# Order of the bias factors, key casts and band copies, and the number of output buffers, in a T5 attention + maxout FFN kernel

## The chip, the cores and the metric

The kernel runs on one core of a Trainium2 chip. The metric is the device time of one execution in microseconds (us). Before the change the median of three executions is 356.96 us, the lowest 355.21 and the highest 357.01.

Names used: PE is TensorE (matmuls and transposes), DVE is VectorE, ACT is ScalarE, POOL is GpSimd, SP is SyncE. SP, ACT and POOL also issue DMAs. PSUM is the memory that matmuls write; SBUF is the working memory.

## The reference

```python
def _attn_ref(q, k, v, bias_table):            # q, k, v: (8, 8, 576, 64) f32, bias_table: (32, 8)
    scores = (1.0 / np.sqrt(D)) * np.matmul(q, k.transpose(0, 1, 3, 2))
    bucket = ...                               # of |i - j|: 0..15 one each, then logarithmic up to 128, then 31
    scores = scores + bias_table[bucket].transpose(2, 0, 1)[None]
    attn = np.exp(scores - np.max(scores, axis=-1, keepdims=True))
    attn = attn / (np.sum(attn, axis=-1, keepdims=True) + 1e-09)
    return np.matmul(attn, v)

def reference(...):
    x = attn_out.transpose(0, 2, 1, 3).reshape(B * S, H * D)          # 4608 x 512
    h = np.maximum(np.maximum(x @ w1, x @ w2), x @ w3)                # 4608 x 768
    return h @ w_out                                                  # 4608 x 512
```

The bias depends on the head and on the distance of query and key alone, and is one constant per head from a distance of about 128 on.

## The kernel before

**The work.** There are 8 batches of 8 heads with 576 queries and keys. Heads go in pairs (`hp` 0 to 3), since two heads of 64 fill the 128 partitions. Keys are cut into 4 blocks of 128 and a rest of 64; queries into two halves of 256 and a rest of 64. One "visit" of a pair and a half (`visit`) makes 8 score matmuls (`sc<-qT,kT`) and two exponentials on ACT (`e<-sc`). `left_keys` (`sct`) and `left_queries` (`scq`) do the rests. `attend` multiplies the exponentials with the values (`a<-vx,e`), and its inner function `quotients` divides by the row sums on DVE and writes `x_sb`.

**The bias.** Instead of adding a bias, the kernel multiplies the exponentials by a factor, exp(bias - last bias), which is 1 away from the diagonal. The 32 x 8 table comes in over ACT's queue as `tableT`; DVE negates its last column (`negc`), ACT makes the factors `etab`, and 17 small DVE copies spread them over `w_sb`, one row per head. ACT stores `w_sb` to DRAM as `w_dr`, and SP reads it back with one shifted row per partition: two loads `hank` (heads 0 to 3, then 4 to 7) and four small ones `hankt`. `make_band` copies a pair's part of `hank` in reverse into `band`; `times_band` multiplies the exponentials near the diagonal by it, three DVE instructions per pair in the first half. `bands(hp)` does both for the first half of batch 0.

**The first batch.** The keys of batch 0 come in f32: heads 0 and 1 (pair 0) over ACT's queue, with the table between the two, heads 2 to 7 over SP's. `cast_keys(hp)` turns a pair's keys to bf16 on DVE. `first_transposes(hp)` transposes the pair's first queries and its keys on PE into a PSUM tile `tp`, and copies them out to `qT` and `kT` (DVE, but ACT for `qT` of pair 0). The first loop over `hp` visits the first query half of each pair and, from pair 1 on, queues the bands of the pair before; at pair 3 it also runs the first `attend`. The second loop visits the second half of batch 0. Then come batches 1 to 7, with two visits per pair.

**The FFN between.** `ffn` cuts a block of 512 tokens into portions of matmuls which `fill` places between the visits of the following batch, so that PE has work while ACT computes exponentials. A portion's three products go to PSUM banks `ps`, are reduced by a maximum (ACT copies the first one, DVE does the two maxima) into `hT`, and `output` multiplies `hT` by `w_out` into a bank `pso`. All of `ps`, `pso` and the transposes of batch 0 share the two banks of the pool `ps_f`. DVE copies `pso` into an SBUF tile `osb` (line 339), whose pool `osbp` has 3 buffers, and SP stores `osb` (line 343). The stores are held back in a list and issued by `store_outputs` after the next visit, so on SP's queue they stand among the DMA transposes of that place (line 405 for the next batch's queries and keys, line 565 for `x_sb`). A block has four outputs, so four copies and four stores.

**What sets the order.** Each engine runs its instructions in one fixed order. Calls wrapped in `inorder` keep the order of the program; for the others a scheduler places the instruction by its priority. DVE, ACT and SP each work through their list strictly: an instruction that waits holds up all behind it.

```python
    osbp = ctx.enter_context(tc.tile_pool(name="osbp", bufs=3))                      # line 83
    load_32(k, 0, k32, nc.scalar)
    inorder(nc.scalar.dma_start(out=tableT[:], in_=tbl_src))                         # line 193
    load_32(k, 1, k32, nc.scalar)
    last_keys = first_transposes(0)
    inorder(nc.scalar.dma_start(out=w_dr[:], in_=w_sb[:]))                           # line 598
```

Of the kernel before, what the change touches and what calls it, by code (L numbers as in the profile page):

```python
# [39 lines left out]
def kernel(  # L40
# [12 lines left out]
    nc = tc.nc  # L53
# [6 lines left out]
    HP = H // 2  # L60
# [19 lines left out]
    nrm = ctx.enter_context(tc.tile_pool(name="nrm", bufs=3))  # L80
    xs = ctx.enter_context(tc.tile_pool(name="xs", bufs=2))
    ffnw = ctx.enter_context(tc.tile_pool(name="ffnw", bufs=2))
    osbp = ctx.enter_context(tc.tile_pool(name="osbp", bufs=3))
    ps_s = ctx.enter_context(tc.tile_pool(name="ps_s", bufs=2, space=bass.MemoryType.PSUM))
    ps_a = ctx.enter_context(tc.tile_pool(name="ps_a", bufs=2, space=bass.MemoryType.PSUM))
    ps_f = ctx.enter_context(tc.tile_pool(name="ps_f", bufs=2, space=bass.MemoryType.PSUM))
# [4 lines left out]
    inorder = tc.keep_in_program_order  # L91
# [4 lines left out]
    def tr(*args):  # L96
        inorder(nc.tensor.transpose(*args))
# [14 lines left out]
    def act_copy(out_, in_):  # L112
        inorder(nc.scalar.activation(out=out_, in_=in_, func=ACTF.Copy))

    def dve_copy(out_, in_):
        inorder(nc.vector.tensor_copy(out_, in_))  # L116
# [10 lines left out]
    def main_part(src, b):  # L127
        return src[b, :, 0 : KT * P, :].rearrange("h (t p) d -> p t h d", p=P)
# [30 lines left out]
    def load_q(b, h0, h1):  # L159
        load_main(q, b, h0, h1, batch[b][0])  # L160
        load_tail(q, b, h0, h1, q_diag)
# [13 lines left out]
    def borrow(c, n):  # L175
        return xT[:, c, NTOK - 2 * n :].bitcast(F32)

    k32 = borrow(3, KT * H * D).rearrange("p (t h d) -> p t h d", t=KT, h=H)
    q32 = borrow(2, 2 * 2 * D).rearrange("p (t h d) -> p t h d", t=2, h=2)

    def load_32(src, h, dst, eng, nt=KT):
        inorder(eng.dma_start(out=dst[:, :, h, :], in_=main_part(src, 0)[:, 0:nt, h, :]))
# [7 lines left out]
    batch[0] = load_tiles()  # L190
    w_sb = stage.tile([H, WL], BF16, name="w_sb")
    load_32(k, 0, k32, nc.scalar)
    inorder(nc.scalar.dma_start(out=tableT[:], in_=tbl_src))
    load_32(k, 1, k32, nc.scalar)
    nc.scalar.preload_act_table_set("natural_log_exp_and_others")
    for h in range(2):
        load_32(q, h, q32, nc.sync, 2)
    for h in range(2, H):
# [16 lines left out]
        out=negc[:], in0=tableT[:, NB - 1 : NB], scalar1=-1.0, scalar2=None, op0=ALU.mult,  # L215
# [8 lines left out]
    def cast_keys(hp):  # L224
        h = slice(2 * hp, 2 * hp + 2)
        dve_copy(batch[0][1][:, :, h, :], k32[:, :, h, :])
# [5 lines left out]
        mm(warm[:, 0:CH], lhsT=qtail[1][:, 0, :], rhs=qtail[1][:].rearrange("p g c -> p (g c)"))  # L232

    act_copy(batch[0][0][:, 0:2, 0:2, :], q32)
    cast_keys(0)
    dve_copy(w_sb[:, HALF : HALF + single], etab[:, 0:single])
    reach = single
    for vv, rg in enumerate(ranges):
# [7 lines left out]
    w_dr = dram.tile([H, WL], BF16, name="w_dr")  # L246
# [15 lines left out]
    def make_band(hp):  # L262
        dve_copy(band[hp][:], hank[:, 2 * hp : 2 * hp + 2, ::-1])
# [148 lines left out]
    def qk_tiles():  # L412
        return [qkt.tile([P, HP, (KT + 1) * P], BF16, tag=n, name=n) for n in ("qT", "kT")]

    def first_transposes(hp):


        hs = slice(2 * hp, 2 * hp + 2)
        tp = ps_f.tile([P, 2 * CH], BF16, tag="ff", name="tp1")
        K, L = KT * P, KT * P + P  # L420
        for t in range(2):
            tr(tp[:, L + P * t : L + P * t + P], batch[0][0][:, t, hs, :].rearrange("p h d -> p (h d)"), ident[:])
        for t in range(KT):
            tr(tp[:, P * t : P * t + P], batch[0][1][:, t, hs, :].rearrange("p h d -> p (h d)"), ident[:])
        if hp:
            tr(tp[:, K:L], ktail[0][:, hp, :], ident[:])
        (dve_copy if hp else act_copy)(qk[0][0][:, hp, 0:QS], tp[:, L : L + QS])
        if hp:
            dve_copy(qk[0][1][:, hp, :], tp[:, 0:L])
            return  # L430
        dve_copy(qk[0][1][:, hp, 0:K], tp[:, 0:K])

        def last_keys():
            tr(tp[:, K:L], ktail[0][:, hp, :], ident[:])
            dve_copy(qk[0][1][:, hp, K:], tp[:, K:L])
        return last_keys

    def more_transposes(hp):

        hs = slice(2 * hp, 2 * hp + 2)  # L440
        tp = ps_f.tile([P, 2 * CH], BF16, tag="ff", name="tp2")
        for t in range(2):
            tr(tp[:, P * t : P * t + P], batch[0][0][:, 2 + t, hs, :].rearrange("p h d -> p (h d)"), ident[:])
        tr(tp[:, QS : QS + P], qtail[0][:, hp, :], ident[:])
        act_copy(qk[0][0][:, hp, QS:], tp[:, 0 : QS + P])
# [12 lines left out]
    def times_band(hp, e4, t, lo, hi):  # L458
        lo, hi = max(lo, P * t - P), min(hi, P * t + 2 * P)
        if lo < hi:  # L460
            nc.vector.tensor_tensor(  # L461
                out=e4[:, t, :, lo:hi], in0=e4[:, t, :, lo:hi],
                in1=band[hp][:, :, lo - P * t + P : hi - P * t + P], op=ALU.mult,
            )
# [4 lines left out]
    def visit(qT, kT, e4, c, mid=None):  # L469


        for tt in range(0, KT, 2):
            sc = ps_s.tile([P, 2, 2, QS], F32, tag="sc", name="sc")
            for t in range(2):
                for par in range(2):
                    r = slice(64 * par, 64 * par + 64)
                    mm(
                        sc[:, par, t, :], lhsT=kT[r, P * (tt + t) : P * (tt + t) + P],
                        rhs=qT[r, c * QS : c * QS + QS],
                    )  # L480
            exp(e4[:, tt : tt + 2, :, c * QS : c * QS + QS].rearrange("p t h q -> p h t q"), sc[:])
            if tt == 0 and mid:
                mid()

    def left_keys(hp, qT, kT, et, lo, hi, sc=None):


        if sc is None:
            sc = ps_s.tile([P, 2 * CH], F32, tag="sc", name="sct")
        for q0 in range(lo, hi, CH):  # L490
            q1 = min(q0 + CH, hi)
            mm(sc[:, q0 - lo : q1 - lo], lhsT=kT[:, KT * P :], rhs=qT[:, q0:q1])
        exp(et[:, lo:hi], sc[:, 0 : hi - lo])
        if hi > QM:
            nc.vector.tensor_tensor(  # L495
                out=et[:, hi - 256 :], in0=et[:, hi - 256 :], in1=bandt[:, hp, :], op=ALU.mult
            )
# [86 lines left out]
    def next_late():  # L584
        return late.pop(0)() if late else (lambda: None)

    def e_tiles():
        return (
            ep.tile([P, KT, 2, QM], BF16, tag="e4", name="e4"),
            ep.tile([P, KT, 2 * 64], BF16, tag="eq", name="eq"),  # L590
            ep.tile([P, S + 64], BF16, tag="et", name="et"),
        )

    qk = [qk_tiles(), qk_tiles()]
    last_keys = first_transposes(0)
    inorder(nc.scalar.dma_start(out=w_dr[:], in_=w_sb[:]))
    for h0 in (0, KT):
        load_hank(h0, h0 + KT)  # L600
    load_hankt()
# [17 lines left out]
    def bands(hp):  # L619
        make_band(hp)  # L620
        for t in range(KT):
            times_band(hp, first_e[hp], t, 0, QS)
# [4 lines left out]
    for hp in range(HP):  # L627
        qT, kT = (x[:, hp, :] for x in qk[0])
        e4, eq, et = e_tiles()
        first_e.append(e4)  # L630
        visit(qT, kT, e4, 0, (lambda: first_transposes(hp + 1)) if 0 < hp < HP - 1 else None)
        if hp == 0:
            last_keys()
            first_transposes(1)
        if hp + 2 < HP:
            cast_keys(hp + 2)
        if hp:
            bands(hp - 1)
        late.append(lambda hp=hp, e4=e4, eq=eq, et=et: attend(0, hp, e4, eq, et, 0))
        if hp == HP - 1:  # L640
            next_late()()
        left_keys(hp, qT, kT, et, 0, QS, ps_a.tile([P, QS], F32, tag="a", name="sct"))
# [5 lines left out]
    for hp in range(HP):  # L648
        qT, kT = (x[:, hp, :] for x in qk[0])
        e4, eq, et = e_tiles()  # L650
        visit(qT, kT, e4, 1, (lambda: more_transposes(hp + 1)) if hp + 1 < HP else None)
        if hp == 0:
            bands(HP - 1)
            dve_copy(bandt[:], hankt[:, :, ::-1])
        if hp == 2:
            x_transposes(3, 0)
            add_ffn(0, QS)
        quotients = next_late()
        for t in range(KT):
            times_band(hp, e4, t, QS, QM)  # L660
        keys = lambda: left_keys(hp, qT, kT, et, QS, S + 64)
        queries = lambda: left_queries(hp, qT, kT, eq)
        if hp < 2:
            quotients()
            x_transposes(2 * hp, 0)
            keys()
            if hp == 0:
                x_transposes(1, 0)
            queries()
        else:  # L670
            if hp == HP - 1:
                batch[2] = load_tiles()
                load_q(2, 0, H)
                load_k(2, 0, H)
                quotients = lambda q=quotients: (q(), x_transposes(0, 1))
            fill(8, quotients, keys, queries, *([lambda: second_transposes(qk[1], 0)] if hp == HP - 1 else []))
        late.append(lambda hp=hp, e4=e4, eq=eq, et=et: attend(0, hp, e4, eq, et, 1))
# [96 lines left out]
```

## Time and profile before

| | |
|---|---|
| device time, median of 3 (lowest, highest) | 356.96 us (355.21, 357.01) |
| the profiled execution's own time | 358.48 us |
| span of its profile, first to last instruction | 356.7 us |
| mean granted TensorE clock | 0.957 of 2.4 GHz |
| PE busy | 319.9 us (90%) |
| ACT busy | 220.9 us (62%) |
| DVE busy | 210.5 us (59%) |
| chain that ended last: PE / ACT / DVE / DMA | 56% / 14% / 13% / 12% |

The profile is of one execution. Times in its rows are microseconds from the start of the span, durations in us or, where marked, ns. A row of the timeline gives start, duration, engine, line, operation, output<-inputs, shapes and count, and in square brackets how long the engine had been idle and what released it. A row of the chain of waits gives start, duration and what the end hung on. A row of windows gives, for one stretch, its length, then the busy time and count of each engine, then the granted TensorE clock (1.00 is the upper level of 2.4 GHz, 0.50 the lower of 1.2 GHz), the share of the DMA engines and GB/s.

### The profile page before, as it was taken

What the parts mean: (1) busy time and instruction counts of PE and PEld (TensorE: products, weight loads), DVE (VectorE), ACT (ScalarE), POOL (GpSimd) and SP (SyncE); (2) the same over time, 40 slices, a digit from 0 to 9 for tenths busy, and PEclk for the clock granted to TensorE, in tenths of its full rate; (3) what the DMA queues carried; (4) which work ended last, traced back from release to release, by engine and by line L of the source; (5) the groups of instructions that cost most, each with busy time, mean ns of one, the idle gap of its engine ahead of it and who ended that gap; (6) DMA issues with size and microseconds to landing.
All of it is one profiled execution on the core that took longest, in us unless ns stands there. A gap on an engine that the chain in (4) does not pass through costs nothing.

```text
span 356.7 us, 7723 instructions
## 1 busy us (share of the span) xinstructions
PE 319.9 (90%) x3063; PEld 179.1 (50%) x3063; DVE 210.5 (59%) x524; ACT 220.9 (62%) x334; POOL 117.1 (33%) x154
## 2 busy tenths in 40 slices
PE   6707889998999979998999989997999999999995
PEld 2305567677555535554555535563555555544442
DVE  5316666766666645666666636674667666455352
ACT  2707988779677746777677747774777775022221
POOL 8822985348935823713092400050000000000000
PEclk9557999999999998999999989998999999999999
DMA  9999999999999999919798972099502300310203
GB/s 145 159 214 187 98 142 116 133 178 143 184 144 135 164 206 146 134 33 161 165 134 75 124 203 45 17 89 197 102 0 57 130 0 9 105 73 21 97 2 119
DMA packets 172957, 40.90 MB, mean 115 GB/s; under 512 B 164976, under 2 KB 168312, under 8 KB 172920
## 3 DMA queue, kind: packets, MB, share of 16 engines
q0 software_dynamic: 110656, 16.72, 73.8%
q1 hardware_dynamic: 60928, 23.41, 33.7%
q8 instruction: 24, 0.39, 0.5%
q10 hardware_dynamic: 1336, 0.27, 0.4%
q14 instruction: 13, 0.11, 0.1%
HBM read 35.65 MB, written 9.45 MB: 126 GB/s over the span
## 4 chain that ended last, share of the span: by engine, by line
PE 56%; ACT 14%; DVE 13%; DMA 12%; issue 2%; SPq 1%; ACTq 0%; DVEq 0%
PE ps L94 31%; ACT e L467 10%; PE pso L94 8%; PE sc L94 7%; PE a L94 7%; DMA out_dram<-osb 6%; DVE e L461 5%; DMA hank<-w_dr 3%; DVE hT L326 3%; DVE x_sb L548 2%; PE sct L94 2%; DMA w_dr<-w_sb 2%; DMA xT<-in_k_dram 1%; DVE osb L339 1%; ACT m L302 1%
## 5 line engine op out<-in xcount | busy, mean ns | idle before, releaser
L94 PE MATMUL ps<-xT,w_bf 128*128 128x512 bf16 (+1 forms) x720 | 158.2, 361 | 12.1 <-DVE osb L339 8.6
L467 ACT ACTIVATE e<-sc 128x1024 bf16<-128x1024 f32 x128 | 124.8, 1023 | 45.3 <-PE sc L94 45.1
L94 PEld LDWEIGHTS <-w_bf 128*128 128x128 bf16 x720 | 67.3, 98 | 72.3 <-issue 18.1
L461 DVE TENSOR_TENSOR e<-e,band 128x512 bf16<-128x512 bf16 (+2 forms) x136 | 61.7, 466 | 34.8 <-ACT e L467 34.3
L302 ACT ACTIVATE m<-ps 128x512 bf16<-128x512 f32 x54 | 32.2, 597 | 52.2 <-PE ps L94 50.4
L94 PEld LDWEIGHTS <-kT 64*128 64x128 bf16 (+1 forms) x704 | 36.2, 96 | 56.0 <-issue 28.1
L94 PE MATMUL sc<-qT,kT 64*128 64x256 bf16 x512 | 43.8, 283 | 15.1 <-DVE kT L116 12.3
L94 PE MATMUL pso<-wo_bf,hT 128*128 128x512 bf16 x216 | 51.4, 379 | 0.5 <-DVE hT L326 0.5
L321 DVE TENSOR_TENSOR m<-ps,m 128x512 bf16<-128x512 f32 x54 | 37.2, 688 | 21.3 <-ACT m L302 14.5
L94 PE MATMUL a<-vx,e 128*128 128x65 bf16 x1024 | 47.0, 196 | 0.0
L140 POOL DMA_DIRECT2D q_sb<-in_q_dram x32 | 28.2, 910 | 46.8 <-DMA qT<-q_sb 43.4
L94 PEld LDWEIGHTS <-e 128*128 128x128 bf16 x1024 | 42.7, 100 | 1.1 <-issue 0.3
L326 DVE TENSOR_TENSOR hT<-ps,m 128x512 bf16<-128x512 f32 x54 | 37.0, 686 | 4.6 <-PE ps L94 3.1
L94 PE MATMUL a<-vt,et 128*128 128x130 bf16 x160 | 36.4, 228 | 0.5 <-DVE x_sb L548 0.4
L339 DVE COPY osb<-pso 128x512 f32<-128x512 f32 x32 | 22.1, 691 | 19.1 <-DMA out_dram<-osb 10.2
L94 PEld LDWEIGHTS <-hT 128*128 128x128 bf16 x216 | 19.8, 98 | 21.5 <-DVE hT L326 1.5
L140 POOL DMA_DIRECT2D vx<-in_v_dram x32 | 28.5, 922 | 4.3 <-PE a L94 2.7
L548 DVE TENSOR_TENSOR x_sb<-a,rd 128x256 bf16<-128x256 f32 x64 | 27.1, 424 | 2.0
L557 ACT ACTIVATE x_sb<-a,rd 64x64 bf16<-64x64 f32 x64 | 19.8, 309 | 13.6 <-DVE x_sb L548 11.6
L157 POOL DMA_DIRECT2D vt<-in_v_dram x16 | 10.5, 670 | 50.0 <-PE a L94 50.0
L495 DVE TENSOR_TENSOR et<-et,bandt 128x256 bf16<-128x256 bf16 x32 | 9.3, 291 | 29.3 <-ACT et L467 29.3
L140 POOL DMA_DIRECT2D k_sb<-in_k_dram x28 | 24.7, 916 | 5.1 <-DMA wo_bf<-in_moe_w_out_dram 4.5
(56 smaller groups left out, 208.8 us busy)
## 6 DMA issues: line engine op xcount, KB each, us to landing
out_dram<-osb SPq DMA_DIRECT2D x36, 256.0 KB, 2.5
vx<-in_v_dram POOLq DMA_DIRECT2D x32, 128.0 KB, 6.4
q_sb<-in_q_dram POOLq DMA_DIRECT2D x26, 128.0 KB, 5.0
k_sb<-in_k_dram POOLq DMA_DIRECT2D x24, 128.0 KB, 5.7
w_bf<-in_moe_w_dram POOLq DMA_DIRECT2D x3, 768.0 KB, 11.9
xT<-in_k_dram SPq DMA_DIRECT2D x6, 128.0 KB, 5.9
hank<-w_dr SPq DMA_DIRECT2D x2, 384.0 KB, 12.8
wo_bf<-in_moe_w_out_dram POOLq DMA_DIRECT2D x1, 768.0 KB, 10.8
```

The lines of the kernel that those rows point to most:

```text
L94: inorder(nc.tensor.matmul(*args, **kw))
L140: nc.gpsimd.dma_start(out=dst[:, t, h0:h1, :], in_=x[:, t, h0:h1, :])
L157: nc.gpsimd.dma_start(out=dst(b, par, h0, h1), in_=tail_part(src, b, h0, h1, par))
L302: nc.scalar.activation(out=st[fb]["m0"][:], in_=st[fb]["ps0"], func=ACTF.Copy)
L321: nc.vector.tensor_tensor(out=m[:], in0=st[fb]["ps1"], in1=st[fb]["m0"][:], op=ALU.max)
L326: nc.vector.tensor_tensor(out=hT[:, fb * CH : fb * CH + CH], in0=ps2, in1=st[fb]["m"][:], op=ALU.max)
L339: nc.vector.tensor_copy(osb[:], ps[:])
L461: nc.vector.tensor_tensor(out=e4[:, t, :, lo:hi], in0=e4[:, t, :, lo:hi], in1=band[hp][:, :, lo - P * t + P : hi - P * t + P], op=ALU.mult,)
L467: nc.scalar.activation(out=out_, in_=in_, func=ACTF.Exp, scale=inv_sqrt_d)
L495: nc.vector.tensor_tensor(out=et[:, hi - 256 :], in0=et[:, hi - 256 :], in1=bandt[:, hp, :], op=ALU.mult)
L548: nc.vector.tensor_tensor(out=x_sb[b][:, 2 * half : 2 * half + 2, f].rearrange("p t (h d) -> p t h d", d=D), in0=x[:, 0:4, 0:D].rearrange( ...
L557: nc.scalar.activation(out=x_sb[b][0:64, KT, P * hp + 64 * par : P * hp + 64 * par + 64], in_=x[r, 4 + par, 0:D], func=ACTF.Copy, scale=rd ...
```

## The change

Four edits:

- The output pool `osbp` gets 6 buffers in place of 3.
- On ACT's queue the table is loaded behind both key loads instead of between them.
- On DVE the cast of the first keys stands behind the 17 copies into `w_sb`, and on ACT the store of `w_sb` stands ahead of the copy of `qT` of pair 0.
- The bands of each pair are queued one pair later: `bands(0)` and `bands(1)` in the first loop at pairs 2 and 3, `bands(2)` and `bands(3)` at the first pair of the second loop.

```diff
-    osbp = ctx.enter_context(tc.tile_pool(name="osbp", bufs=3))
+    osbp = ctx.enter_context(tc.tile_pool(name="osbp", bufs=6))
...
     load_32(k, 0, k32, nc.scalar)
+    load_32(k, 1, k32, nc.scalar)
     inorder(nc.scalar.dma_start(out=tableT[:], in_=tbl_src))
-    load_32(k, 1, k32, nc.scalar)
...
     act_copy(batch[0][0][:, 0:2, 0:2, :], q32)
-    cast_keys(0)
     dve_copy(w_sb[:, HALF : HALF + single], etab[:, 0:single])
...
     qk = [qk_tiles(), qk_tiles()]
+    inorder(nc.scalar.dma_start(out=w_dr[:], in_=w_sb[:]))
+    cast_keys(0)
     last_keys = first_transposes(0)
-    inorder(nc.scalar.dma_start(out=w_dr[:], in_=w_sb[:]))
...
         if hp + 2 < HP:
             cast_keys(hp + 2)
-        if hp:
-            bands(hp - 1)
+        if hp > 1:
+            bands(hp - 2)
...
         if hp == 0:
+            bands(HP - 2)
             bands(HP - 1)
             dve_copy(bandt[:], hankt[:, :, ::-1])
```

**The order on ACT at the start.** `xT<-in_k_dram` are the two f32 key loads of pair 0 (the f32 keys are parked in a part of `xT`). Before:

```order
L182 DMA xT<-in_k_dram 128x4x64
L193 DMA tableT<-in_bias_table_dram 8x32x1
L182 DMA xT<-in_k_dram 128x4x64
L195 ACT_TABLE_LOAD
L218 ACTIVATE etab<-tableT,negc 8x32
L113 ACTIVATE q_sb<-xT 128x2x128
L113 ACTIVATE qT<-tp_197 128x256
L598 DMA w_dr<-w_sb 8x511
```

and now:

```order
L182 DMA xT<-in_k_dram 128x4x64 x2
L194 DMA tableT<-in_bias_table_dram 8x32x1
L195 ACT_TABLE_LOAD
L218 ACTIVATE etab<-tableT,negc 8x32
L113 ACTIVATE q_sb<-xT 128x2x128
L596 DMA w_dr<-w_sb 8x511
L113 ACTIVATE qT<-tp_198 128x256
```

The table is the third load in place of the second, and the store `w_dr` changed places with the copy of `qT`.

**The order on DVE at the start.** Between `negc` and the first copies into `w_sb` (a minus is a row of the kernel before):

```order
 L125 MEMSET vt_97 64x4 x2
 L214 TENSOR_SCALAR negc<-tableT 8x1
-L116 CAST k_sb<-xT 128x4x128
 L116 COPY w_sb<-etab 8x16
 L116 COPY w_sb<-etab 8x3 x4
 L116 COPY w_sb<-etab 8x4
```

The first cast of keys left this place; it now follows the last copy into `w_sb`.

**The order on DVE around the bands.** `e_247` and `e_278` are the exponentials of pairs 0 and 1, `qT<-tp` and `kT<-tp` the copies for pair 3. Before:

```order
L116 CAST k_sb<-xT 128x4x128
L116 COPY band_187<-hank 128x768
L461 TENSOR_TENSOR e_247<-e_247,band_187 128x2x256 x2
L461 TENSOR_TENSOR e_247<-e_247,band_187 128x2x128
L116 COPY qT<-tp_320 128x256
L116 COPY kT<-tp_320 128x640
L116 COPY band_188<-hank 128x768
L461 TENSOR_TENSOR e_278<-e_278,band_188 128x2x256 x2
L461 TENSOR_TENSOR e_278<-e_278,band_188 128x2x128
L116 COPY band_189<-hank 128x768
```

and now:

```order
L116 CAST k_sb<-xT 128x4x128
L116 COPY qT<-tp_316 128x256
L116 COPY kT<-tp_316 128x640
L116 COPY band_186<-hank 128x768
L460 TENSOR_TENSOR e_247<-e_247,band_186 128x2x256 x2
L460 TENSOR_TENSOR e_247<-e_247,band_186 128x2x128
L116 COPY band_187<-hank 128x768
L460 TENSOR_TENSOR e_278<-e_278,band_187 128x2x256 x2
L460 TENSOR_TENSOR e_278<-e_278,band_187 128x2x128
L545 RECIPROCAL rd<-a 128x4
L547 TENSOR_TENSOR x_sb<-a,rd 128x2x128
```

The two copies for pair 3 moved ahead of the first row that waits for `hank`, and the quotients of the first `attend` moved ahead of the third band.

## Rows read from the trace of the kernel before

**Rows 1.** The page's busy time by engine: us (share of span) xinstructions.
```profile
PE 319.9 (90%) x3063; PEld 179.1 (50%) x3063; DVE 210.5 (59%) x524; ACT 220.9 (62%) x334; POOL 117.1 (33%) x154
```
**Rows 2.** Waits, all engines: who <- for whom: total us, times, longest us.
```profile
PE sc L94 <- DVE kT L116: 12.3, 2, 10.8
...
DVE osb L339 <- DMA out_dram<-osb: 10.2, 5, 2.4
...
PE ps L94 <- DVE osb L339: 8.6, 4, 2.6
```
**Rows 3.** Chain of waits, the start: start us, duration us, what.
```profile
1.25 0.68 ACTq L193
1.96 4.79 DMA xT<-in_k_dram
6.85 0.82 DVE k_sb L116
7.67 1.32 DVE w_sb L116 x16
9.24 5.64 DMA w_dr<-w_sb
14.89 10.39 DMA hank<-w_dr
25.77 0.96 DVE e L461 x3
```
**Rows 4.** Timeline of all engines, the first 32 us.
```profile
4.02 0.14 DVE L214 TENSOR_SCALAR negc<-tableT 8x1 f32<-8x1 f32 x1 [0.32 <-DMA tableT<-in_bias_table_dram]
4.20 0.32 ACT L218 ACTIVATE etab<-tableT,negc 8x32 bf16<-8x32 f32 x1 [0.52 <-DVE negc L214]
...
13.76 0.75 POOL L606 DMA_DIRECT2D w_bf<-in_moe_w_dram  x1 [0.28 <-DMA vx<-in_v_dram]
...
17.20 0.38 ACT L467 ACTIVATE et<-sct 128x256 bf16<-128x256 f32 x1
...
26.85 0.48 DVE L116 COPY kT<-tp 128x640 bf16<-128x640 bf16 x1
...
27.39 1.04 PE L94 MATMUL sc<-qT,kT 64*128 64x256 bf16 x8 [10.83 <-DVE kT L116]
...
28.35 0.29 PE L94 MATMUL a<-vt,et 128*128 128x130 bf16 x1
...
30.47 0.36 DVE L116 COPY band<-hank 128x768 bf16<-128x768 bf16 x1 [1.81 <-DMA hank<-w_dr]
...
31.56 1.02 ACT L467 ACTIVATE e<-sc 128x1024 bf16<-128x1024 f32 x1 [0.87 <-PE sc L94]
```
**Rows 5.** Timeline of PE in batch 3, around the wait for `osb`.
```profile
127.00 1.46 PE L94 MATMUL pso<-wo_bf,hT 128*128 128x512 bf16 x6
...
132.11 1.02 PE L94 MATMUL ps<-xT,w_bf 128*128 128x512 bf16 x4 [2.57 <-DVE osb L339]
```
**Rows 6.** Timeline of DVE, same place.
```profile
131.37 0.69 DVE L339 COPY osb<-pso 128x512 f32<-128x512 f32 x1 [2.40 <-DMA out_dram<-osb]
```
**Rows 7.** Timeline of SP, same place.
```profile
125.71 0.52 SPq L343 DMA_DIRECT2D out_dram<-osb  x1
```
**Rows 8.** Windows: the same 55 matmuls in batches 3, 4, 5, 6 and 7.
```profile
127.00:137.49 10.49, 7.92 (x55) 3.99 (x53) 5.09 (x12) 4.57 (x8) 0.00 (x0) 0.84 1.65 226
165.84:173.65 7.81, 6.38 (x55) 3.24 (x53) 4.75 (x12) 4.58 (x8) 0.00 (x0) 1.00 1.10 217
202.00:212.28 10.28, 7.97 (x55) 3.94 (x53) 5.13 (x12) 4.57 (x8) 0.00 (x0) 0.83 1.18 214
240.63:250.84 10.21, 7.93 (x56) 3.91 (x54) 5.10 (x12) 4.57 (x8) 0.00 (x0) 0.83 1.63 208
279.18:285.64 6.46, 6.38 (x55) 3.22 (x53) 4.68 (x12) 4.58 (x8) 0.00 (x0) 1.00 0.32 121
```
**Rows 9.** Windows: one period, from that place in batch 2 to batch 3.
```profile
92.19:127.00 34.81, 34.48 (x352) 18.77 (x350) 23.20 (x56) 26.11 (x40) 23.67 (x30) 1.00 2.10 152
```

## The prediction

> **What bounds the kernel now.** I read the page's busy times first: PE is busy for 90% of the span and no other engine for more than 62% [rows 1], so time is won where PE waits, or where its matmuls run at the lower clock. The list of waits says where. Two entries stand out: 12.3 us, 10.8 of it in one piece, until a copy of `kT`, and 8.6 us in four pieces until a copy into `osb`; that copy itself waited 10.2 us in five pieces for stores to land [rows 2]. So I looked at two places.
>
> The first is the start. In the chain of waits the program hangs on a single line: table and keys, factors, `w_dr`, `hank`, first band [rows 3]. While `hank` is under way, from 14.89 to 25.28, PE has nothing to do, because the `kT` copy of pair 3 (26.85) stands on DVE behind the band copy that waits for `hank`; PE sits idle for 10.83 us until 27.39 [rows 4].
>
> The second is a place that recurs once in each of batches 3 to 6. SP issues the store of the first output late (125.71, behind transposes of `x_sb`) [rows 7]. The fourth copy needs that store's buffer, so DVE stands still for 2.40 us [rows 6]. The bank that this copy would free is wanted by PE's next product, which comes after 2.57 us of idleness [rows 5]. To see the full price I cut the same 55 matmuls, from the last `pso` of the block to the `sct` of the next visit, out of five batches [rows 8]. Batch 7 has no wait there and takes 6.46 us at a granted clock of 1.00. The others take 10.49, 7.81, 10.28 and 10.21. In three of them the matmuls themselves are slower too: 7.92 to 7.97 us busy against 6.38, at a mean clock of 0.83 or 0.84. After the idle stretches of over 2 us the clock fell to the lower level for part of the window; after the one of 1.43 us it stayed at 1.00.
>
> **Six output buffers.** A block makes four copies, so with six buffers a copy takes one that was last filled six copies earlier, in the block before the last or in the last block's second half, a period of some 35 us back [rows 9]; its store has landed long since. The wait of DVE goes, and with it PE's. The gain is each window minus batch 7's: 4.03 + 1.35 + 3.82 + 3.75 = **12.95 us**. Of it 8.27 are idle time (2.57 + 1.43 + 2.31 + 2.28, less 0.08 in each window) and 4.68 are the lower clock. The bounds: 7.8 if only DVE's own waits go (10.2, less a fifth piece that no wait of PE answers to, of 2.4 us at most) and PE meets something else; 12.95 if nothing else is late. I take the upper end, because one whole period without this wait exists: from batch 2 to batch 3 it takes 34.81 us at clock 1.00 with PE busy for 34.48, while POOL issues loads for 23.67 us [rows 9]. Loads, transposes and stores keep up at that pace; what comes next is PE's own work. The fifth wait of DVE, near the end, I cost at nothing, since PE has none beside it.
>
> **Table behind the keys, factors ahead of the cast.** Now the table lands before 4.02 and its factors are ready at 4.52 (4.20 + 0.32) [rows 4], but DVE first waits for the keys (landed at 1.96 + 4.79 = 6.75) and casts them for 0.82; the copies into `w_sb` end just before the store is issued at 9.24 [rows 3]. After the change nothing of the keys stands ahead. From the table's arrival to the store it takes 0.5 for `negc` and `etab` and 1.57 for the copies (7.67 to 9.24), say 2.2 with handovers. What is unknown is when a table that stands third on its queue lands. Its issue starts somewhere between the second and the third place of now, 1.25 and 1.96, say at 1.7. With its own old time to arrival, 2.77 us (1.25 to 4.02), it lands at 4.5, and the store leaves at 6.7, 2.5 earlier. At the other end it lands when the second key load did, at 6.75; the store leaves at 8.95, 0.3 earlier. The third place took 4.79 us for a far larger load, so I take the middle, 5.6: the store leaves at 7.8, **1.4 us** earlier, and I pass this on to `hank` one to one.
>
> The Trainium skill (DMA: Bandwidth & Descriptors, Queues, rings and completion order) says that on each DMA engine the descriptors of a ring are consumed in ring order. The trace agrees so far: the table, then second, was there 2.7 us before the keys behind it. By that rule the table cannot pass the keys; the sum would use the end of 0.3.
>
> The price is that the cast of pair 0 starts at about 7.8 in place of 6.85, so everything up to the first exponentials is 0.9 us later. This is hidden: the work that the first loop could do ended at 17.58 (17.20 + 0.38) [rows 4], pair 3's score matmuls (1.04) and two exponentials (about 2) now follow it, which makes 21.5 at most with the delay, and `hank` is not there before 23.9. If `hank` came three us sooner than that, this cover would be gone. On ACT the copy of `qT` is now behind the store and waits with it; the copy of `kT` that it serves is not ready earlier.
>
> **Bands behind the transpose copies.** The `kT` copy of pair 3 no longer waits, so 1.04 us of matmuls and their exponentials move into the idle stretch. Measured from the landing of `hank`, the first `attend` (28.35 before) starts when the first band's products are done, at 26.73: 1.6 us sooner. That is the upper bound, if ACT's first exponential of the second loop (31.56) follows in step. The lower bound is nothing: the third band waits for the second `hank` load (30.47) [rows 4], which this edit does not move, and whatever hangs on that band gains nothing. The second loop hangs on both, so I take the middle, **0.8 us**. The two bands that moved into the second loop cost what they cost before; DVE had gaps there.
>
> **The sum.** 12.95 + 1.4 + 0.8 = 15.15 us. The profiled execution took 358.48 us, so the change gives 343.3 by its own time. The median of the three timed runs is 1.5 us lower, which gives 341.8. Whether those runs waited less at these very places is not known; I forecast the middle, **342.6 us**.
>
> **Rivals.**
> 1. *The table comes last on its ring.* It lands at 6.75, and the start gains 0.3 + 0.8. Time 343.7. For it: the order on the queue. Against: its size. Chance 0.16.
> 2. *`hank` overtakes the weight loads.* POOL issues the first FFN weights at 13.76 [rows 4], 1.1 us before `hank` is issued. With the store 1.4 earlier, `hank` goes ahead of them, and its 10.39 us, spent beside them, could shrink by some 2.5, a quarter. Time 340. Against: other loads fill the DMA engines before. Chance 0.12.
> 3. *Another wait takes the place of the stores.* Once the copy is prompt, PE could meet the next batch's transposes, which SP issues behind the same stores, and keep part of the pause with its clock loss. Only 7.8 of the 12.95 remain: 347.7. Against: the period of 34.81. Chance 0.08.
> 4. *More buffers do nothing.* If the copy waits for its turn on DVE and not for a store, only the start gains, 2.2: 355.5 or so, next to no change. Against: the row names the store, and batch 7, whose blocks are the same, copies without delay. Chance 0.03.
> 5. *Slower.* The table, now behind everything, becomes the start's bound: DVE's first row waits for it, and so do all keys, since the casts stand behind. Each us that it lands after 7.0 (where the store would leave at 9.2, as now) costs one. To eat up the 13.75 of the other parts it must land after about 21 us, and for a clear loss after 22.5: 359 or more. Against: no load of the first microseconds took so long; the key load took 4.79. Chance 0.03.
>
> **How the numbers follow.** The forecast has 0.58, and its own range is 340 to 345.5 (the start's two terms between their bounds, 0.3 to 4.1 us together, and half of the 1.5 us between median and profiled run to either side). The rivals have the rest. A range of 338.5 to 347.0 takes in rivals 1 and 2 and leaves 3, 4 and 5 out, 0.14. A change of 0.5%, 1.8 us, is about what a measurement of this kernel can tell from none. Faster by more: the forecast and rivals 1 to 3, 0.94. Within: rival 4, 0.03. Slower: rival 5, 0.03.
>
> **What would show it.** In the profile after: no wait of DVE for `out_dram<-osb` in batches 3 to 6, and the five windows all near 6.46 at clock 1.00. The store of `w_dr` near 7.8 and `hank` near 23.9. The score matmuls of pair 3 before `hank` lands, and PE released next by the first band's products. The prediction is wrong if a batch's period stays 3 to 4 us above 34.8, if PE waits for `qT` or `kT` at a batch's first visit, or if the first band is not earlier than 25.

## The result and the profile after

| | before | after |
|---|---|---|
| median (lowest to highest; executions) | 356.99 us (355.21 to 358.3; 4) | 345.43 us (344.52 to 346.41; 4) |
| profiled execution, its span | 358.48 us, 356.7 us | 344.52 us, 342.8 us |

The ratio is 0.968 with a 95% interval of 0.9629 to 0.9731: the change makes the kernel 3.2% faster. The forecast was 342.6 with a range of 338.5 to 347.0; the sign and the range were right, the point was 2.8 us too low. By the two profiled spans the gain is 13.9 us, where the sum said 15.15. Of the four executions behind the 340.51 us at the end of part 4, one (344.09) counts as slow and is left out of the ratio given there; the median of the other three is 338.97.

The page after, its busy line and chain, answers to [rows 1]:

```profile
PE 314.3 (92%) x3022; PEld 177.7 (52%) x3063; DVE 209.7 (61%) x524; ACT 221.0 (64%) x334; POOL 117.2 (34%) x154
...
PEclk9566999999999999999999999999999999999999
...
PE 60%; DVE 15%; ACT 14%; DMA 7%; issue 2%; ACTq 0%; DVEq 0%
```

DVE and ACT do what they did. PE shows 5.6 us less, but 41 of its matmul records are missing from this trace (x3022 against x3063); six buffers alone (part 1 below), with all 3063, shows 317.2, 2.7 less than before. From the fifth slice on the clock is at the upper level. The waits of after at the start, to be read beside [rows 2] (who <- for whom: total us, times, longest us):

```profile
DVE band L116 <- DMA hank<-w_dr: 7.2, 1, 7.2
PE a L94 <- DVE e L460: 6.7, 1, 6.7
...
DVE negc L214 <- DMA tableT<-in_bias_table_dram: 2.9, 1, 2.9
```

The list has no wait of DVE for `out_dram` any more and none of PE for `osb`; before they were 10.2 and 8.6 us. The place of [rows 5 to 8] in batches 3 to 6, and the period from batch 2 to batch 3, first as windows (length, busy time and count of PE, PEld, DVE, ACT, POOL, then clock, DMA share, GB/s):

```profile
126.02:132.48 6.46, 6.27 (x54) 3.23 (x53) 4.68 (x12) 4.58 (x8) 0.00 (x0) 1.00 1.52 257
160.82:167.28 6.46, 6.33 (x54) 3.23 (x53) 4.68 (x12) 4.58 (x8) 0.00 (x0) 1.00 1.36 229
195.62:202.08 6.46, 6.32 (x54) 3.24 (x53) 4.68 (x12) 4.58 (x8) 0.00 (x0) 1.00 1.49 191
230.43:236.89 6.46, 6.33 (x55) 3.24 (x54) 4.68 (x12) 4.57 (x8) 0.00 (x0) 1.00 1.78 179
...
91.21:126.02 34.81, 34.21 (x346) 18.79 (x349) 23.17 (x56) 26.12 (x40) 19.70 (x25) 1.00 2.04 148
```

and DVE and SP in batch 3, timeline:

```profile
127.91 0.68 DVE L338 COPY osb<-pso 128x512 f32<-128x512 f32 x1
```
```profile
124.63 0.59 SPq L342 DMA_DIRECT2D out_dram<-osb  x1
```

All four windows are 6.46 us at clock 1.00, to the hundredth what batch 7 took before, and the period is still 34.81. SP issues the store as late as before [rows 7]; it has merely stopped mattering, since the copy needs no buffer back.

Where the 13.9 us came from can be read at one matmul. The fourth group of `pso` of batch 2, ahead of all four places, starts at 92.19 before [rows 9] and at 91.21 after. So in this pair of profiles **the start gave 1.0 us, and the four places 12.9**, against 2.2 and 12.95 in the sum. The 1.0 can't be laid to the edits: with the old start and six buffers (part 1) that matmul came at 91.45, with the new start and four buffers (part 5) at 92.36. The start after, timeline of all engines, answers to [rows 4]:

```profile
1.84 0.65 ACTq L194 DMA_DIRECT2D tableT<-in_bias_table_dram  x1
6.58 0.14 DVE L214 TENSOR_SCALAR negc<-tableT 8x1 f32<-8x1 f32 x1 [2.88 <-DMA tableT<-in_bias_table_dram]
...
8.98 0.30 ACTq L596 DMA_DIRECT2D w_dr<-w_sb  x1
...
14.39 0.92 SPq L249 DMA_DIRECT2D hank<-w_dr  x2
...
18.12 0.59 PE L94 MATMUL sc<-qT,kT 64*128 64x256 bf16 x4
...
25.27 0.36 DVE L116 COPY band<-hank 128x768 bf16<-128x768 bf16 x1 [7.22 <-DMA hank<-w_dr]
...
26.22 0.90 PE L94 MATMUL a<-vx,e 128*128 128x65 bf16 x8 [6.68 <-DVE e L460]
...
34.19 0.43 DVE L116 COPY bandt<-hankt 128x1024 bf16<-128x1024 bf16 x1 [0.92 <-DMA hankt<-w_dr]
```

The table lands near 6.5, not 5.6, so the store of `w_dr` leaves 0.26 us earlier (9.24 before), `hank` is issued 0.50 earlier (14.89 before), and the first band is copied when it was before (25.27 against 25.30). Pair 3's score matmuls did move into the idle stretch, and PE's pause shrank from 10.83 to 6.68 us; the time did not follow.

### The profile page after: what moved, and what is told of

It is laid out like the page before. It is cut to its first block, busy times and chain, and to the rows that moved or that the text cites. A ratio compares the mean times of both kernels' runs of the same rounds, so it can differ in the third digit from the quotient of the medians.

```text
span 342.8 us, 7677 instructions
## 1 busy us (share of the span) xinstructions
PE 314.3 (92%) x3022; PEld 177.7 (52%) x3063; DVE 209.7 (61%) x524; ACT 221.0 (64%) x334; POOL 117.2 (34%) x154
## 4 chain that ended last, share of the span: by engine, by line
PE 60%; DVE 15%; ACT 14%; DMA 7%; issue 2%; ACTq 0%; DVEq 0%
PE ps L94 31%; PE pso L94 11%; ACT e L466 11%; PE sc L94 8%; PE a L94 7%; DVE e L460 7%; DMA hank<-w_dr 3%; DVE x_sb L547 3%; DVE hT L325 3%; DMA xT<-in_k_dram 2%; PE sct L94 2%; DMA w_dr<-w_sb 2%; DVE osb L338 1%; ACT m L301 1%; ACT eq L466 1%
## 5 line engine op out<-in xcount | busy, mean ns | idle before, releaser
L94 PE MATMUL ps<-xT,w_bf 128*128 128x512 bf16 (+1 forms) x695 | 152.8, 357 | 5.2 <-ACT m L301 1.2
L94 PE MATMUL pso<-wo_bf,hT 128*128 128x512 bf16 x200 | 49.1, 379 | 1.3 <-DVE hT L325 0.8
L94 PEld LDWEIGHTS <-e 128*128 128x128 bf16 x1024 | 41.8, 99 | 8.1 <-DVE e L460 7.3
L466 ACT ACTIVATE et<-sct 128x640 bf16<-128x640 f32 (+2 forms) x36 | 23.2, 645 | 9.4 <-PE sct L94 9.4
L556 ACT ACTIVATE x_sb<-a,rd 64x64 bf16<-64x64 f32 x64 | 19.9, 310 | 13.6 <-DVE x_sb L547 11.6
## 6 DMA issues: line engine op xcount, KB each, us to landing
hank<-w_dr SPq DMA_DIRECT2D x2, 384.0 KB, 10.9
```

What stands on the lines that cost most here:

```text
L94: inorder(nc.tensor.matmul(*args, **kw))
L466: nc.scalar.activation(out=out_, in_=in_, func=ACTF.Exp, scale=inv_sqrt_d)
L556: nc.scalar.activation(out=x_sb[b][0:64, KT, P * hp + 64 * par : P * hp + 64 * par + 64], in_=x[r, 4 + par, 0:D], func=ACTF.Copy, scale=rd ...
```

## The experiments

The theories that the expectations name: **A**, the buffers give the 12.9 and the start's edits next to nothing; **B**, the start's edits carry several us. Then, for the start: **C**, its gate is the last `hankt` load, whose copy `bandt` stands ahead of the second loop; **D**, its gate is `hank` and the first band. **A1** says that other transfers decide when `hank` lands, **A2** that `hank` follows the store at a fixed distance. **E**, the FFN weight loads that POOL issues meanwhile slow these transfers; **F**, they don't. All ratios are to the kernel before, run beside each.

**1. The parts alone.** The kernel before with six buffers and nothing else:

```diff
-    osbp = ctx.enter_context(tc.tile_pool(name="osbp", bufs=3))
+    osbp = ctx.enter_context(tc.tile_pool(name="osbp", bufs=6))
```

> The kernel before with six output buffers and nothing else. Theory A (of the 13.9 us that the profile's span lost, 12.9 come from the buffers, about 1.0 from the place of the bands, and the order of table and cast gave nothing): a span near 343.8, a time some 1 us above the changed kernel's, no wait of DVE for a store, and PE still idle for 10.8 us before the score matmuls of pair 3. Theory B (the start's edits carry several us and the buffers only DVE's own wait, 7.8): a time of 349 or more.

345.38 us (ratio 0.9701, 0.9656 to 0.9745), span 343.9, and no wait of DVE for a store: the one number gives the whole gain of the change, 11.6 us by the medians in both. One detail of A missed: PE's pause was 6.9 us, not 10.8, because `hank` landed earlier in this profile.

The changed kernel with three buffers:

```diff
-    osbp = ctx.enter_context(tc.tile_pool(name="osbp", bufs=6))
+    osbp = ctx.enter_context(tc.tile_pool(name="osbp", bufs=3))
```

> The changed kernel with three output buffers. Theory A: a span near 355.7, the four waits for stores are back, and the time is within 1.5 us of the kernel before. Theory B: at least 3 us below the kernel before.

354.91 us (0.9953, 0.9919 to 0.9987; 10 executions against 13). All three edits of the start together are worth 0.5%, some 1.7 us, with an interval from 0.5 to 2.9; with six buffers nothing of it shows (345.43 against 345.38). Its waits show the four stalls back:

```profile
PE ps L94 <- DVE osb L338: 9.0, 4, 3.1
DVE osb L338 <- DMA out_dram<-osb: 8.3, 4, 2.9
```

Its span of 353.2 lies below the 355.7 that A expected, and mostly not by the start: the `pso` of batch 2 is 0.6 us earlier than before (91.56). The stalls were cheaper in this profile. Cut as in [rows 8], the four windows take 8.51, 8.02, 10.87 and 8.53 us, 10.1 above 6.46 in place of 12.95. The mean clock is lower in the third alone (0.84), where PE had stood idle for 3.06 us; behind 1.64, 2.13 and 2.15 us it stayed at 1.00. So the lost clock in the 12.95 is that of one execution.

Theory A holds, B falls. The changed kernel with table and cast as before (buffers and bands alone):

```diff
     load_32(k, 0, k32, nc.scalar)
-    load_32(k, 1, k32, nc.scalar)
     inorder(nc.scalar.dma_start(out=tableT[:], in_=tbl_src))
+    load_32(k, 1, k32, nc.scalar)
...
     act_copy(batch[0][0][:, 0:2, 0:2, :], q32)
+    cast_keys(0)
...
-    inorder(nc.scalar.dma_start(out=w_dr[:], in_=w_sb[:]))
-    cast_keys(0)
     last_keys = first_transposes(0)
+    inorder(nc.scalar.dma_start(out=w_dr[:], in_=w_sb[:]))
```

> The changed kernel with the table between the keys and the first cast ahead of the factors, as before; bands and buffers stay as changed. Theory A: hank lands at 25.3 as in both kernels, and the time is that of the changed kernel within 0.5 us. Theory B: hank lands later or the first bands are late, and the time is 1 us or more above the changed kernel's.

345.95 us (0.9718, 0.9673 to 0.9763): the same time as the change, within what can be told.

**2. The table between the keys, the factors still first.** The change moved the table back by one place and the cast behind the factors. Here only the second stays:

```diff
     load_32(k, 0, k32, nc.scalar)
-    load_32(k, 1, k32, nc.scalar)
     inorder(nc.scalar.dma_start(out=tableT[:], in_=tbl_src))
+    load_32(k, 1, k32, nc.scalar)
```

> The changed kernel with the table loaded between the two key loads, as before; the factors stay ahead of the cast. The table should land at about 4.0 and the store of the factors leave at about 6.5, 2.5 us earlier than in the changed kernel. Theory A1 (other transfers on the DMA engines decide when hank lands): hank lands within 1 us of 25.3 and the time is that of the changed kernel. Theory A2 (the path from store to hank is a fixed 16 us, as the prediction took it): hank lands near 22.8 and the time is 2 us or more below the changed kernel's.

**342.04 us** (0.9595, 0.9556 to 0.9634): all four executions lie below the lowest of either kernel, though the interval just touches that of the change (from 0.9629). Timeline of its start:

```profile
4.03 0.14 DVE L214 TENSOR_SCALAR negc<-tableT 8x1 f32<-8x1 f32 x1 [0.32 <-DMA tableT<-in_bias_table_dram]
...
6.80 0.31 ACTq L596 DMA_DIRECT2D w_dr<-w_sb  x1
...
12.25 0.93 SPq L249 DMA_DIRECT2D hank<-w_dr  x2
...
13.70 0.80 POOL L606 DMA_DIRECT2D w_bf<-in_moe_w_dram  x1 [0.27 <-DMA vx<-in_v_dram]
...
18.13 0.42 DVE L116 COPY band<-hank 128x768 bf16<-128x768 bf16 x1 [2.18 <-DMA hank<-w_dr]
...
29.37 0.43 DVE L116 COPY bandt<-hankt 128x1024 bf16<-128x1024 bf16 x1 [3.16 <-issue]
```

The table lands 2.5 us before its time in after, and the store leaves 2.2 earlier. `hank` is now issued ahead of the weight loads (12.25 against 13.70) and lands 5.9 us after its issue, where it took 10.9 behind them (14.39 against 13.30 in after). The first band is 7.1 us earlier, but `bandt` only 4.8, and the `pso` of batch 2 (87.17) 4.0. Neither A1 (25.3) nor A2 (22.8) has this `hank`; A2 has the sign of the time, but 5 of the 7.1 us are `hank`'s own, which A2 held fixed. The trace names no releaser for `bandt` here (`issue`); the last `hankt` load, issued at 15.3 and at most 14.0 us under way, landed by about 29.3. Read with part 1: factors first is worth 3.9 us (345.95 to 342.04), and the table's new place gives 3.4 of them back (to 345.43), though these last two were not measured side by side.

**3. What the second loop hangs on.** From the profiled runs: by how much POOL's first weight load is issued ahead of `hank`, the us from the issue of `hank` to the first band (which waits for it in all of them), the starts of that band, of the copy `bandt` and of the `pso` of batch 2, and the difference of the last two:

| kernel | weights ahead by | `hank` takes | first band | `bandt` | `pso` | `pso` - `bandt` |
|---|---|---|---|---|---|---|
| before | 1.13 | 10.4 | 25.30 | 34.98 | 92.19 | 57.21 |
| after | 1.09 | 10.9 | 25.27 | 34.19 | 91.21 | 57.02 |
| three buffers | 0.74 | 10.3 | 24.85 | 34.70 | 91.56 | 56.86 |
| bands and buffers | 0.68 | 9.7 | 24.50 | 34.91 | 92.77 | 57.86 |
| six buffers alone | 0.44 | 6.9 | 21.90 | 34.44 | 91.45 | 57.01 |
| four buffers (5.) | 0.02 | 5.5 | 19.72 | 34.12 | 92.36 | 58.24 |
| bands first (5.) | -0.50 | 4.7 | 19.32 | 30.95 | 88.99 | 58.04 |
| table between | -1.45 | 5.9 | 18.13 | 29.37 | 87.17 | 57.80 |
| between, bands first (5.) | -1.93 | 6.3 | 18.54 | 30.02 | 87.02 | 57.00 |
| between, weights later (4.) | -4.80 | 6.1 | 18.31 | 26.29 | 84.74 | 58.45 |

Two things stand in it. How long `hank` takes goes with the race against the weight loads: 10 us or so when they are issued 0.7 us or more ahead, 7 or less otherwise. One version that is not in the table, `bandt` later (below), departs from this: 0.42 us ahead, and 9.7. No run changes this race alone, so for `hank` it is a correlation. And the end follows `bandt`: the last column varies by 1.6 us, the first band by 7.2. With four buffers the first band came 5.6 us earlier than in after and nothing came of it, because `bandt` stood still:

```profile
19.72 0.36 DVE L116 COPY band<-hank 128x768 bf16<-128x768 bf16 x1 [1.38 <-DMA hank<-w_dr]
...
34.12 0.43 DVE L116 COPY bandt<-hankt 128x1024 bf16<-128x1024 bf16 x1 [5.24 <-DMA hankt<-w_dr]
```

There the wait for `hankt` only moved the pause: PE stood idle until 35.88 for 3.79 us, and from 36 to 40 its clock was 0.50, where in after it was 1.00. The last row is the converse: first band as with the table between, `bandt` 3.1 us earlier, `pso` 2.4 earlier. So C, not D. To test it by an edit, `bandt` and its products went behind the second pair's visit of the second loop, in the changed kernel:

```diff
...
         if hp == 0:
             bands(HP - 2)
             bands(HP - 1)
-            dve_copy(bandt[:], hankt[:, :, ::-1])
...
-        keys = lambda: left_keys(hp, qT, kT, et, QS, S + 64)
+        keys = lambda: left_keys(hp, qT, kT, et, QS, S + 64, mul=hp > 1)
...
+            if hp == 0:
+                et_first = et
+            else:
+                dve_copy(bandt[:], hankt[:, :, ::-1])
+                times_bandt(0, et_first, S + 64)
+                times_bandt(1, et, S + 64)
```

> The changed kernel with the copy bandt<-hankt and the first two products with it moved from the first to the second pair of the second loop, so that DVE no longer stands at the landing of hankt. Theory C (the last hankt load, not the first hank load, is the gate of the second loop: the last pso of batch 2 came 57 us after the copy of bandt, within 1 us, in all six profiles): that pso comes 1 us or more before 91.2 and the time falls by 0.5 to 2 us. Theory D (the gate is hank and the band of the first pair, as the prediction took it): no change, within 0.5 us.

343.3 us (0.9618, 0.9568 to 0.9668), 2.1 below after; no wait for `hankt` is left (`bandt` at 36.83, without one), and `pso` comes at 90.14, 1.1 earlier. That speaks for C only weakly: the intervals overlap, and the first band came 1.5 us earlier too (23.75), so D would have it as well.

The same with the table between:

> The fourth experiment (table between the keys) with the same move of bandt. Theory C: with hank at about 18 and the wait of 3.2 us for hankt gone, another 1 to 3 us below the fourth experiment, at 339 to 341. Theory D: no change from it, 342.

341.42 us (0.9551, 0.9492 to 0.961), `pso` at 84.84, 2.3 earlier than with the table between alone, with a first band 0.5 later (18.64): in these profiles this edit tells C from D. Yet the time is only 0.6 lower, where C expected 1 to 3. PE has a new wait, of 2.3 us, for `xT<-x_sb`, SP's transposes of batch 1's result for the FFN.

**4. The weight loads.** With the table between, the three weight loads moved on POOL's queue behind the first query and key loads of batch 1:

```diff
-    for i, wk in enumerate((moe_w1, moe_w2, moe_w3)):
-        ...
...
+            for i, wk in enumerate((moe_w1, moe_w2, moe_w3)):
+                ...
```

> The fourth experiment with the three FFN weight loads issued on POOL behind the queries and keys of the first two heads of batch 1 instead of ahead of them. Theory E (hank and hankt take 6 to 17 us to land because the weight loads share the DMA engines with them): the copy of bandt comes 2 us or more before 29.4 and the time falls by 1 to 3 us, if the weights still land before the first FFN product. Theory F (hank and hankt are slow by themselves): bandt stays near 29.4 and the time does not fall.

The transfers did what E says. The tile `hankt` (issues: ns each min/median/max, first and last start; then us from issue to landing, min/median/max), in after, with the table between, and here:

```profile
L270 SPq DMA_DIRECT2D hankt<-w_dr x4: 735/2538/2890, 15.4 to 21.3; - x4
...
DMA to landing us min/median/max: 12.8/15.7/17.3
```
```profile
L270 SPq DMA_DIRECT2D hankt<-w_dr x4: 641/668/806, 13.2 to 15.3; - x4
...
DMA to landing us min/median/max: 9.0/11.5/14.0
```
```profile
L270 SPq DMA_DIRECT2D hankt<-w_dr x4: 628/658/692, 13.2 to 15.3; - x4
...
DMA to landing us min/median/max: 7.3/7.6/7.7
```

In after, behind the weight loads, SP needs up to 2.9 us to issue one of the four, and they land after 12.8 or more. With the table between, the weights start among them: 0.8 us at most, and 9.0 to 14.0. With the weights behind all four they land after 7.3 to 7.7; this last step is the edit alone. `bandt` is copied at 26.29 without waiting, and `pso` comes at 84.74, 2.4 earlier than with the table between alone. But the time is 342.18 us (0.9581, 0.9526 to 0.9637): nothing gained, against the 1 to 3 us expected. The profile says where it went, again to the transposes for the FFN, 4 us further on:

```profile
88.89 1.02 PE L94 MATMUL ps<-xT,w_bf 128*128 128x512 bf16 x4 [2.68 <-DMA xT<-x_sb]
```

The clock fell as well, to a mean of 0.85 from 88.80 to 100: from the `pso` of batch 2 to that of batch 3 (123.72) it took 38.98 us, 4.2 above the undisturbed period.

Both moves together:

> The fourth experiment with both moves. Theories C and E: what one move leaves the other takes, and the sum is no more than the larger of the two gains plus 1 us, since both shorten the same wait: 338.5 to 341. If neither holds, 342.

**340.51 us** (0.9541, 0.945 to 0.9632), span 337.1, `pso` at 84.57 and no wait for `xT`: SP's five transposes took 6.0 to 6.6 us to land here, 7.9 to 10.0 in the two runs that waited. Why they were quicker here is open. These four versions (table between alone, and with either or both moves), 340.5 to 342.2, can't be told apart by their intervals. Every execution of them lies below the lowest of after, 344.52, but of the intervals only that with `bandt` later and the weights in place lies clear of after's.

**5. The rest of the change.** Four buffers in the changed kernel (`bufs=6` to `bufs=4`):

> The changed kernel with four output buffers in place of six. A block makes four copies, and the copy that used to wait is its fourth. Theory A (a copy needs no buffer of its own block): four do what six do; time as the changed kernel (345.4), no wait of VectorE for a store in batches 3 to 6. Rival: the stores of the block before, or of the second half of the last visit, are still under way when the next block begins, and part of the four stalls comes back; up to 355 as with three.

344.77 us (0.9659, 0.9593 to 0.9724), and no wait for a store: four do what six do.

The bands as before, in the changed kernel:

```diff
-        if hp > 1:
-            bands(hp - 2)
+        if hp:
+            bands(hp - 1)
...
-            bands(HP - 2)
             bands(HP - 1)
```

> The changed kernel with the band copies back ahead of the transpose copies (each pair's bands queued as before the change); the table, the factors and the six buffers stay. If the band order carries the 0.8 that the prediction gave it, 346.2, and TensorE's long wait for the copy of the keys is back (about 8 to 11 us). Theory C (the second loop hangs on the last hankt load): the long wait comes back, yet the time stays at 345.4, since hankt lands when it lands.

344.46 us (0.9658, 0.9589 to 0.9727). PE's wait for `kT` came back, but short, since `hank` happened to land at 19.3:

```profile
PE sc L94 <- DVE kT L116: 4.6, 3, 3.1
```

So this run did not meet the late `hank` that the order was meant for. Part 1 has a second comparison: bands and buffers (345.95) differs from six buffers alone (345.38) by the bands' order only, and is no faster. The order of the bands has no worth that can be measured here. The same with the table between:

> The version with the table between the two key loads, with the band copies ahead of the transpose copies as before the change. Here hank lands early (first band near 18.1) and VectorE waits only 2 us for it. If the band order matters at all, it matters little: 342.0 within 1; the copies of pair 3's queries and keys wait about 2 us more. Rival: the wait for hank holds up pair 3's transposes, and the loop is 1 to 2 us later, 343 to 344.

344.22 us (0.9627, 0.9554 to 0.97), where the rival said 343 to 344. The median is 2.2 above the version with the bands behind (342.04), but its four executions reach from 341.08 to 344.43 and the intervals overlap; the `pso` of its profile came at 87.02, as there. Whether the bands' order is worth something once `hank` is early stays open.

Last, the best version with the table ahead of both keys:

```diff
+    inorder(nc.scalar.dma_start(out=tableT[:], in_=tbl_src))
     load_32(k, 0, k32, nc.scalar)
-    inorder(nc.scalar.dma_start(out=tableT[:], in_=tbl_src))
     load_32(k, 1, k32, nc.scalar)
```

> The version with the later hankt copy and the later weight loads, with the table moved ahead of both key loads on ScalarE's queue. If the table's place still sets the start, the table lands 0.7 sooner (one issue, 0.68 us), the store of the factors leaves about 0.7 sooner, and the time falls from 340.5 to 339.8 at best. Rival: the keys, one place later, delay the first transposes and exponentials by 0.7, and the time stays or rises to 341.2; TensorE's first score matmuls tell.

340.6 us (0.9578, 0.949 to 0.9665): the time stays, as the rival said, but not for its reason, since PE's first score matmuls start at 9.06 in both versions. The store left at 5.99, 0.8 earlier, and `pso` came at 84.57, where it was. The table is no longer what the start hangs on.

## Why the prediction was right, and where it was not

- **Six buffers, 12.95.** Right in mechanism, and in size for this pair of profiles: 12.9. That three of the four stalls lost clock was chance in the profile before: with three buffers and the new start it was one of four, and 10.1 us. The windows fell to batch 7's 6.46 at clock 1.00, as the cut of [rows 8] said, and the kernel before with this edit alone is as fast as the whole change. Taking the upper bound was justified by the undisturbed period [rows 9]; four buffers would have done, as the sentence that a block makes four copies already implied. (With six, a block's third and fourth copy go back to the first half of the block before, not the second as the prediction says; that is only further back.)
- **Table and factors, 1.4.** Too high. The step that failed first is "so I take the middle, 5.6": the table landed near 6.5, and the store left at 8.98. This is rival 1 (6.75 and 8.95), which had 0.16. The rule of the Trainium skill that stood beside it (DMA: Bandwidth & Descriptors, Queues, rings and completion order) agrees with this trace: between the keys the table was there at 4.02, behind both at 6.5. The same section of the Trainium skill adds that a later transfer may finish its write before an earlier one, so the rule alone does not say that the table cannot pass the keys, as the prediction has it.
- **"I pass this on to `hank` one to one."** The step that failed next. `hank` was issued 0.50 earlier and landed when it had, while the weight loads too came 0.46 earlier (13.30 against 13.76) and stayed 1.1 us ahead. In the table of part 3 its duration goes with that race, which no run tested by itself. Rival 2 described this; it did not happen in after, and does with the table between, where 10.9 us fall to 5.9.
- **Bands, 0.8.** The mechanism showed: pair 3's scores ran at 18.12, PE's pause fell by 4.1 us, and PE was released by the first band's products. The size did not: with the old order the time was the same (344.46; and 345.38 against 345.95). PE's pause began at 16.56 (27.39 less 10.83), not at 14.89, where the prediction has it. "The second loop hangs on both" `hank` loads is the failed step. It hangs on the third transfer, `hankt`, which had no term: `bandt` waited for it 0.92 us in after, and the `pso` of batch 2 follows its copy by 57 to 58 us.
- **The price of the later cast.** Hidden, as said. The first exponentials came at 11.46 in place of 10.03, 1.4 later rather than 0.9, and the first loop's last one ended at 21.0, before `hank`.
- **The point.** 345.43 less 342.6 is 2.8: 1.2 from the start's terms, 0.7 since the forecast took half of the gap between median and profiled run off, and 0.9 since after's profiled execution lies below its median instead of above it. The forecast's own range of 340 to 345.5 just held it; added up again from its terms that range ends at 345.3 (342.6 + 1.9 + 0.75), a little below the measured time. That the total came out near is owed to the one large term. By its own tests, the first band at 25.27 was not earlier than 25: the start's argument was wrong, and small enough not to matter.

## What to carry to other kernels

Price a recurring stall by cutting the same instructions out of one period that has it and one that has not; idle time and lost clock both come out, and that term held to 0.1 us in the same pair of profiles. Take the lost clock as one execution's: it came to 4.7 us over four stalls in one profile and was seen behind one stall of four in another. For a chain through several transfers, look for the last one that the next stage needs and ask what it shares the DMA engines with, before passing an earlier issue on one to one. A small table that heads a long chain belongs ahead of the larger loads on its queue; moved behind them it cost 3.4 us here by the medians.

## What the runs showed that was not expected

- About a microsecond in the issue of the weight loads (1.09 us ahead in after, 0.02 with four buffers) goes with five in the duration of `hank` (10.9 and 5.5): with the store of `w_dr` at 8.97 to 9.24 in seven of the kernels, the first band came anywhere from 19.3 to 25.3. Kernels that differ in nothing there (four buffers and after) fell on either side, so one profile of this start is one sample.
- The issue took longer as well when larger loads were ahead: in after, with the weight loads ahead, one `hankt` issue on SP's queue took up to 2.9 us; with the weights behind all four, 0.7.
- An earlier start met a wait that no profile of the first two kernels had: once `pso` of batch 2 came before 85, the FFN's transposes were 2.3 and 2.7 us late in two of four versions, which gave back what had been won.
